# Part of weight 2 moved into the first attention phase, with buffers and first signs re-placed

## The chip, the cores and the metric

The kernel runs on one core of a Trainium2 chip. The metric is device microseconds of one execution, from the first to the last instruction plus what lies around that span. TensorE (PE) multiplies matrices; VectorE (DVE), ScalarE (ACT) and GpSimd (POOL) do the elementwise work; SyncE (SP) issues every DMA of this kernel, plain copies and transposes alike, in one queue. Each engine runs its instructions in the order of its own list and stops at the first whose inputs or buffers aren't ready. "PEld" in the profile is TensorE's weight load.

## The reference, cut to what matters

Three layers in a row, for 2 batches of 768 rows. First an attention of 8 heads of size 64 in which a query sees only the keys of its own hash bucket, then a low-rank token mix with a ReLU layer of 512 to 2048 to 512, then a causal attention by 4 experts with a top-2 gate.

```
q_bits = (q @ proj > 0); k_bits = (k @ proj > 0)          # 6 bits each
mask = bucket(q_bits) == bucket(k_bits)
x = softmax(where(mask, scale * q @ k.T, -1e9)) @ v       # layer 1, heads joined: 512 wide
u = x + (x.T @ U @ V).T
x = u + relu(u @ w_ch1) @ w_ch2                           # layer 2; w_ch1 512 x 2048, w_ch2 2048 x 512
out = sum_e gate_e * (causal_softmax(q_e @ k_e.T) @ v_e @ wo_e)   # layer 3
```

The weights U, V, w_ch1 and w_ch2 arrive as 64-bit floats, which the kernel reads as pairs of 32-bit words.

## The kernel before

Numbers that need more than half precision are kept as two half-precision parts, a high and a low one, so most products take three matmuls.

**Layer 1** goes by pairs of heads (two heads share the 128 partitions), 4 pairs in each batch, and in a pair by 12 tiles of 128 queries x 768 keys: 48 tiles a batch, counted here as tiles 0 to 47 (batch 0) and 48 to 95 (batch 1). In a tile TensorE makes the scores (L607, and L612 with the mask), VectorE takes the row minimum out of PSUM into `P32` (L618), ScalarE takes the exponential (L527), ScalarE or VectorE rounds it to the high half (L529, L531), GpSimd or VectorE subtracts for the low half (L535), SyncE transposes both by DMA into `PT` (L629), and TensorE multiplies with V (L539 to L541). In batch 0 every other tile takes another way: it stays in 32 bits and is transposed on TensorE (`softmax_f32`). The mask comes from sign bits: proj times q and k gives 24 rows of signs for each head, scaled to a large number, which lie in partitions 64 to 87 of `BQ` and `BK` beside the low halves in partitions 0 to 63. `a1_prep` makes the next pair's operands; `a1_first` makes the first pair's by a shorter way: two sign products stand in PSUM partitions 0 to 63, VectorE compares them into `SG` (L516), and SyncE copies 24 rows each to partition 64 and up of `BQ` (L519) and `BK` (L520), for each of the two heads.

**The weights** w_ch1 and w_ch2 come in 16 units each of 128 x 512 numbers. A unit is one DMA of 512 KB (L276), three VectorE operations from 64-bit words to a 32-bit float (L187, L190, L193), one ScalarE operation for the high half (L279) and two on GpSimd for the low half (L280, L281). `w_stream` interleaves the first `NW0` = 16 units (all of weight 1) with tiles 0 to 47 of attention and up to `NW1` = 17 with the 8 tiles after; `need`, called by the first block of the ReLU layer with the numbers in `WAH`, calls for the other 15.

**Space.** Weight 2's place, two tiles of 16 KB a partition (tags `W2_0`, `W2_1`), can't be filled while batch 0's attention runs, since `more_buffers` lends it to attention: 3 further `P32`, 3 `HL`, 2 `PT` and 2 V buffers, besides the 3 each of `P32`, `HL` and `PT` that are there all the time.

**The ReLU layer** (`mlp_stream`) goes by blocks of 256 or 128 rows: 16 products `ph` (L738) with ReLU into `hT` (L739, L740), then 4 products `px` (L758) with weight 2, each followed by a sum on VectorE (L766 to L771). Its blocks of batch 0 are filler for TensorE between the attention tiles of batch 1 (`merge`, `MIX`, `LEAD`).

**The order.** The program text gives priorities; a scheduler with a model of time then writes each engine's list once, when the kernel is built. So an edit of a few lines moves instructions on all engines.

Of the kernel before, what the change touches and what calls it, by code (L numbers as in the profile page):

```python
# [1 line left out]

# [1 line left out]

# [18 lines left out]
def kernel(  # L23
# [17 lines left out]
    nc = tc.nc  # L41
# [30 lines left out]
    IS1 = None
    IS2 = None
    IS3 = None
    IS4 = None
# [5 lines left out]
    W4 = 1.0  # L81
    SOON = 20
    XB = 1
    WAH = (4, 8, 4)
    XNB = 1
    LAGX = 1
    LAGB = 4
# [23 lines left out]
    def halves(n):  # L111
        return [(c, min(512, n - c)) for c in range(0, n, 512)]
# [130 lines left out]


    W1 = [cp.tile([P, ND, FF], FH, name=f"W1_{i}") for i in range(2)]
    W2 = []


    U1 = []
# [54 lines left out]

    M2 = {}
# [36 lines left out]
    def later(n, fn):  # L342
        pending.append([n, fn])
# [113 lines left out]
    def a1_first(b, p):  # L457
# [14 lines left out]
        def turned(src, name):  # L472
# [2 lines left out]
                nc.tensor.transpose(tp[:, t, :], src[:, t, :], identh)  # L475
            return tp

        for j in range(2):
            todo[2 * j]()
            todo[2 * j + 1]()  # L480
            if j == 0:
                load_proj()
        rows = slice(D, D + NR)
        for j in range(2):
            g = slice(NT * j, NT * (j + 1))
            lo = KL[:, :, D * j : D * (j + 1)]
# [12 lines left out]
            tk = turned(KN[:, g], f"tk_{n}_{j}")
            nc.vector.tensor_copy(AK[:, j], tk)  # L500
            tl = turned(lo, f"tl_{n}_{j}")
            nc.scalar.activation(BK[0:D, j], tl, AF.Copy)
            sg = psc.tile([D, 1024], F32, tag="sc", name=f"sg_{n}_{j}")
            for c0, cn in halves(S):
                cs = slice(c0, c0 + cn)
                for last, ops in enumerate((
                    ((PQ, AQ[:, j]), (PK, AK[:, j])),
                    ((PL, AQ[:, j]), (PB[0:D, 0], BK[0:D, j])),
                )):
# [50 lines left out]
    def more_buffers(on):  # L560
        for x in ring.values():
            x.clear()
        if on:
            raw = []
            for i in range(2):
                x = sp.tile([P, 5, S], F32, tag=f"W2_{i}", name=f"more{i}")
                raw += [x[:, j] for j in range(5)]
            half = lambda x, s_: x.bitcast(FH).rearrange("p (a s) -> p a s", s=s_)
            ring["P32"] += raw[0:3]
            ring["HL"] += [half(x, S) for x in raw[3:6]]  # L570
            ring["PT"] += [half(x, P) for x in raw[6:8]]
            VF.extend(x.rearrange("p (t d) -> p t d", d=D) for x in raw[8:10])
# [118 lines left out]
    def a1_stream():  # L691
        pairs = [(b, p) for b in range(B) for p in range(NP)]
        for i, (b, p) in enumerate(pairs):
# [10 lines left out]

            if i == 0:
                later(2, ahead)
                def luv():
                    with tc.issue_after(masked[IS4]) if IS4 is not None else nullcontext():
                        load_uv()
                later(4, luv)  # L710
# [10 lines left out]
    def mlp_stream(b, s0, TB):  # L721
# [350 lines left out]
    def merge(*a):  # L1072
        drain(merged(*a))
# [4 lines left out]

    more_buffers(True)
    a1_first(0, 0)  # L1080
    with tc.issue_after(masked[IS2]) if IS2 is not None else nullcontext():
        for fn in a1_load(0, 1, False):
            fn()

    wunits = [lambda dt=dt, c=c: w1_unit(dt, c) for c in range(FF // 512) for dt in range(ND)]
    wunits += [lambda dt=dt, g=g: w2_unit(dt, g) for dt in range(ND) for g in range(NF // 4)]

    def need(n):
        while given[0] < min(n, len(wunits)):
            with tc.issue_after(masked[IS3]) if IS3 is not None and given[0] < 8 else nullcontext():  # L1090
                wunits[given[0]]()
# [118 lines left out]
```

## Time and profile before

| | us |
|---|---|
| three runs | 654.06, 654.67, 655.4 (median 654.67) |
| profiled execution, whole | 652.22 |
| its span | 650.5 |
| TensorE busy in the span | 577.4 (89%) |
| VectorE busy | 425.9 (65%) |
| ScalarE busy | 347.9 (53%) |
| GpSimd busy | 235.8 (36%) |
| hardware DMA queue, share of 16 engines | 62.3% |

The profile shows one execution. A busy share over the whole span mixes two very different parts: up to about 263 us the attention of layer 1 and the conversion of weights run, with four engines and the DMA much in use; after it TensorE is nearly always busy. So the trace is read by stretches here.

### The profile page before, as it was taken

Reading aid. Unit: us, or ns where it says so; the run is one execution under the profiler, and the core shown is the slowest. Engines: PE = TensorE matmul, PEld = TensorE weight load, DVE = VectorE, ACT = ScalarE, POOL = GpSimd, SP = SyncE. Lnnn points to the kernel's source line nnn. Section 1 sums busy time; section 2 is a strip of 40 time slices with the busy share of each in tenths; the row PEclk is TensorE's granted clock in tenths of the full one; section 3 lists DMA queues with packets and bytes.
Section 4 is the critical chain, followed back from the end, with each engine's and each line's share of the span. In section 5 each row is a group of like instructions: output and inputs, shape, how many; then the busy total and the mean of one; then the engine's idle time right before and its main releaser. Section 6 shows DMA issues by size and latency. Waiting matters only on the chain.

```text
span 650.5 us, 16196 instructions
## 1 busy us (share of the span) xinstructions
PE 577.4 (89%) x6498; PEld 470.1 (72%) x6498; DVE 425.9 (65%) x1030; ACT 347.9 (53%) x744; POOL 235.8 (36%) x215
## 2 busy tenths in 40 slices
PE   5679898796788969989998999999998999998994
PEld 2357677584666659876787888878786888987953
DVE  6886986958978974666765455673772436374295
ACT  4578694865867552684666343452532323354263
POOL 3665776674875773262343200010130000011031
PEclk9999997797999989999999999999998999999998
DMA  8899999969899998495766312251451102026044
GB/s 236 183 208 204 226 219 222 245 134 269 170 230 267 250 217 151 83 195 107 123 122 100 72 30 49 47 108 31 80 89 46 38 10 38 26 46 110 11 100 106
DMA packets 228172, 84.51 MB, mean 130 GB/s; under 512 B 207104, under 2 KB 223616, under 8 KB 228096
## 3 DMA queue, kind: packets, MB, share of 16 engines
q1 hardware_dynamic: 228096, 83.47, 62.3%
q8 instruction: 51, 0.84, 0.5%
q14 instruction: 25, 0.20, 0.1%
HBM read 29.11 MB, written 3.15 MB: 50 GB/s over the span
## 4 chain that ended last, share of the span: by engine, by line
PE 50%; DMA 22%; DVE 10%; POOL 6%; SPq 5%; issue 4%; ACT 3%; DVEq 0%; POOLq 0%; ACTq 0%
DMA PT<-HL 14%; PE ph L738 14%; PE px L758 13%; PE pq L809 2%; PE pk L809 2%; PE s L912 2%; PE po L591 2%; PE pv L841 2%; POOL HL L535 2%; DVE P L618 2%; PE sc L607 2%; DMA more<-HL 1%; SPq L629 1%; PE sc L612 1%; DMA w<-in_moe_w_ch_dram 1%
## 5 line engine op out<-in xcount | busy, mean ns | idle before, releaser
L535 POOL TENSOR_TENSOR HL<-P,HL 128x768 f16<-128x768 f32 (+5 forms) x59 | 86.2, 1462 | 315.7 <-DVE HL L531 180.6
L758 PE MATMUL px<-hT,W 128*128 128x256 f16 (+1 forms) x1344 | 145.2, 259 | 5.1 <-DVE x L766 5.1
L738 PE MATMUL ph<-U,W 128*128 128x256 f16 (+1 forms) x1344 | 144.3, 259 | 0.8 <-DVE hT L740 0.7
L758 PEld LDWEIGHTS <-W 128*128 128x128 f16 x1344 | 115.2, 98 | 20.5 <-issue 6.8
L738 PEld LDWEIGHTS <-W 128*128 128x128 f16 x1344 | 114.9, 98 | 17.1 <-issue 1.9
L527 ACT ACTIVATE P<-P,m 128x768 f32<-128x768 f32 (+5 forms) x103 | 83.0, 806 | 57.1 <-DVE P L920 28.4
L618 DVE TENSOR_SCALAR_CACHE_REDUCE P<-sc 128x768 f32<-128x768 f32 x72 | 68.2, 950 | 12.4 <-PE sc L612 8.7
L740 DVE SCALAR_TENSOR_TENSOR hT<-ph,hT 128x256 f16<-128x256 f32 (+1 forms) x112 | 42.4, 382 | 49.2 <-ACT hT L739 48.6
L539 PEld LDWEIGHTS <-PT 128*128 128x128 f16 x516 | 47.2, 99 | 30.9 <-DMA PT<-HL 25.2
L739 ACT ACTIVATE hT<-ph 128x256 f16<-128x256 f32 (+1 forms) x112 | 38.6, 346 | 57.6 <-PE ph L738 57.0
L529 ACT ACTIVATE HL<-P 128x768 f16<-128x768 f32 (+5 forms) x75 | 56.4, 752 | 18.7 <-DMA PT<-HL 17.7
L607 PE MATMUL sc<-AK,AQ 128*128 128x512 f16 x192 | 50.6, 345 | 14.5 <-DVE more L618 6.2
L539 PE MATMUL po<-V,PT 128*128 128x64 f16 x372 | 41.5, 196 | 12.3 <-DMA PT<-HL 9.0
L612 PE MATMUL sc<-BK,BQ 88*128 88x512 f16 x192 | 50.9, 346 | 0.0
L540 PEld LDWEIGHTS <-PT 128*128 128x128 f16 x516 | 47.2, 99 | 2.0 <-issue 1.1
L541 PEld LDWEIGHTS <-PT 128*128 128x128 f16 x516 | 47.2, 99 | 0.2 <-issue 0.2
L541 PE MATMUL po<-V,PT 128*128 128x64 f16 x372 | 41.5, 195 | 0.0
L540 PE MATMUL po<-V,PT 128*128 128x64 f16 x372 | 41.2, 195 | 0.0
L535 DVE TENSOR_TENSOR HL<-P,HL 128x768 f16<-128x768 f32 (+5 forms) x40 | 34.3, 858 | 9.9 <-ACT HL L529 9.4
L920 DVE TENSOR_SCALAR_CACHE_REDUCE P<-s 128x128 f32<-128x128 f32 (+5 forms) x48 | 29.4, 618 | 10.0 <-PE s L917 9.8
L607 PEld LDWEIGHTS <-AQ 128*128 128x128 f16 x192 | 18.5, 105 | 22.7 <-issue 19.1
L612 PEld LDWEIGHTS <-BQ 88*128 88x128 f16 x192 | 19.7, 103 | 13.9 <-issue 2.8
(238 smaller groups left out, 1181.3 us busy)
## 6 DMA issues: line engine op xcount, KB each, us to landing
w<-in_moe_w_ch_dram SPq DMA_DIRECT2D x16, 512.0 KB
wx<-in_moe_w_ch_dram SPq DMA_DIRECT2D x16, 512.0 KB
qn<-in_q_dram SPq DMA_DIRECT2D x16, 192.0 KB
kn<-in_k_dram SPq DMA_DIRECT2D x16, 192.0 KB
vn<-in_v_dram SPq DMA_DIRECT2D x16, 192.0 KB
out_dram<-o SPq DMA_DIRECT2D x12, 256.0 KB
PT<-HL SPq DMA_TRANSPOSE x99
BQ<-AQ SPq DMA_DIRECT2D x7, 192.0 KB
```

Of the source, the lines that this page charges most:

```text
L527: nc.scalar.activation(P32, P32, AF.Exp, bias=m, scale=-1.0, accum_out=ssum)
L529: nc.scalar.activation(HL[:, 0], P32, AF.Copy)
L535: eng.tensor_tensor(HL[:, 1], P32, HL[:, 0], op=ALU.subtract)
L539: nc.tensor.matmul(o, PT[:, t, :], vh(t), start=(t == 0), stop=False)
L540: nc.tensor.matmul(o, PT[:, t, :], vl(t), start=False, stop=False)
L541: nc.tensor.matmul(o, PT[:, nk + t, :], vh(t), start=False, stop=(t == nk - 1))
L607: nc.tensor.matmul(ps[:, c0 : c0 + cn], aq[:, t, :], ak[:, c0 : c0 + cn], start=True, stop=False,)
L612: nc.tensor.matmul(ps[:, c0 : c0 + cn], bq[:, t, :], bk[:, c0 : c0 + cn], start=False, stop=True,)
L618: nc.vector.tensor_scalar(P32, ps[:, 0:S], CLIP, None, op0=ALU.min, op1=ALU.min, accum_out=m)
L738: nc.tensor.matmul(ph, w, u, start=(i == 0), stop=(i == len(ops) - 1))
L740: nc.vector.scalar_tensor_tensor(hT[1][:, ft, :], ph, 0.0, hT[0][:, ft, :], op0=ALU.max, op1=ALU.subtract)
L758: nc.tensor.matmul(po, w, u, start=(i == 0), stop=(i == len(ops) - 1))
```

## The change

Five edits. (1) In `a1_first` the sign products of q and of k become two products, each written to PSUM partitions 64 to 95, and VectorE compares 24 rows of each straight into `BQ` and `BK`; `SG` and the four copies by DMA are gone. (2) In `a1_prep` the second half of `KN`, a scaled copy, goes from VectorE (L407 before) to GpSimd (L404 after). (3) Weight 2 is split into two pairs of tiles by output column (`W2[0]` and `W2[1]`, 8 units each); the first pair has a place of its own. (4) `more_buffers` lends only the second pair's place and that of `hT`: 2 `P32`, 2 `HL`, 2 `PT` and 2 V buffers. (5) `NWA` = 24 units instead of 16 go with tiles 0 to 47, up to 25 with the next 8 tiles, and the last 7 by `WAH` = (1, 7, 0). The `IS1` to `IS4` switches, all None before, and the place of `load_proj` in the text are clean-up.

```diff
-    WAH = (4, 8, 4)
+    WAH = (1, 7, 0)
...
     def w2_unit(dt, g):
-        if not W2:
-            W2.extend(
-                sp.tile([P, ND, NF, P], FH, tag=f"W2_{i}", name=f"W2_{i}") for i in range(2)
-            )
+        if dt // 2 not in W2:
+            W2[dt // 2] = [
+                sp.tile([P, 2, NF, P], FH, tag=f"W2_{i}_{dt // 2}", name=f"W2_{i}_{dt // 2}")
+                for i in range(2)
+            ]
...
-        nc.vector.tensor_scalar(
-            KN[:, :, D : 2 * D], KN[:, :, 0:D], -0.125, None, op0=ALU.mult
+        nc.gpsimd.tensor_scalar(
+            KN[:, :, D : 2 * D], KN[:, :, 0:D], -0.125, 1.0, op0=ALU.mult, op1=ALU.mult
         )
...
-            sg = psc.tile([D, 1024], F32, tag="sc", name=f"sg_{n}_{j}")
-            for c0, cn in halves(S):
...
-            SG = sp.tile([D, NT, P], FH, tag="KS", bufs=2, name=f"SG_{n}_{j}")
-            nc.vector.tensor_scalar(
-                f2(SG), sg[:, 0:S], thr[0:D, 1:2], far[0:D, 1:2], op0=ALU.is_lt, op1=ALU.mult
-            )
-            nc.sync.dma_start(BQ[rows, j], SG[0:NR])
-            masked.append(nc.sync.dma_start(BK[rows, j], SG[32 : 32 + NR]).ins)
+            for kind, c, ops in (
+                ("q", 1, ((PQ, AQ[:, j]), (PL, AQ[:, j]))),
+                ("k", 0, ((PK, AK[:, j]), (PB[0:D, 0], BK[0:D, j]))),
+            ):
+                sg = psc.tile([P, 1024], F32, tag="sc", name=f"sg{kind}_{n}_{j}")
+                for c0, cn in halves(S):
                     for i, (w, x) in enumerate(ops):
                         nc.tensor.matmul(
+                            sg[D : D + 32, c0 : c0 + cn], w, f2(x)[:, c0 : c0 + cn],
+                            start=(i == 0), stop=(i == 1),
                         )
+                B = BQ if kind == "q" else BK
+                nc.vector.tensor_scalar(
+                    f2(B[rows, j]), sg[rows, 0:S], thr[rows, c : c + 1], far[rows, c : c + 1],
+                    op0=ALU.is_lt, op1=ALU.mult,
+                )
...
-            for i in range(2):
-                x = sp.tile([P, 5, S], F32, tag=f"W2_{i}", name=f"more{i}")
-                raw += [x[:, j] for j in range(5)]
+            for tag in ("W2_0_1", "W2_1_1", "hT0", "hT1"):
+                x = sp.tile([P, 2, S], F32, tag=tag, name=f"more_{tag}")
+                raw += [x[:, j] for j in range(2)]
...
-    NW1 = 17
+    NWA = 24
+    NW1 = 25
...
-    merge(take(a1, NF1), NF1 * CA, w_stream(NW0), NW0)
-    merge(take(a1, PH1 - NF1), (PH1 - NF1) * CA, w_stream(NW1), NW1 - NW0)
+    merge(take(a1, NF1), NF1 * CA, w_stream(NWA), NWA)
+    merge(take(a1, PH1 - NF1), (PH1 - NF1) * CA, w_stream(NW1), NW1 - NWA)
```

Three places in the lists that the scheduler wrote. In them a name such as `w2_3_1` is weight 2's unit of output column block 3 and row group 1 (`_x`, `_32` and `wx` are its staging), `m_1_1_0_5` is the row minimum of batch 1, pair 1, head 0, tile 5, and `us`, `uf`, `vs` belong to the low-rank matrices.

VectorE at the start, from the second sign comparison of the first pair up to tile 0, in the kernel before:

```order
L516 TENSOR_SCALAR SG_0_0_1_243<-sg_0_0_1_234,thr_98,far_99 64x768
L187 TENSOR_SCALAR us_x_416<-us_413 128x192
L190 SCALAR_TENSOR_TENSOR us_x_416<-us_413,us_x_416 128x192
L193 SCALAR_TENSOR_TENSOR uf_415<-us_413,us_x_416 128x192
L208 SCALAR_TENSOR_TENSOR UU1_124<-uf_415,UU0_123 128x6x32
L231 COPY UU0_123<-UU0_123 128x6x32 x2
L231 COPY UU1_124<-UU1_124 128x6x32 x2
L402 SCALAR_TENSOR_TENSOR QN_0_1_329<-QN_0_1_329,qn_0_1_252 128x12x64
L407 TENSOR_SCALAR KN_0_1_330<-KN_0_1_330 128x12x64
L187 TENSOR_SCALAR vs0_x_431<-vs0_426 96x384
L618 TENSOR_SCALAR more0_128,m_0_0_0_0_269<-sc_0_0_0_0_264 128x768
```

The same stretch in the changed kernel, from the first sign comparison:

```order
L512 TENSOR_SCALAR BQ_0_0_140<-sgq_0_0_0_193,thr_98,far_99 24x768
L512 TENSOR_SCALAR BK_0_0_141<-sgk_0_0_0_199,thr_98,far_99 24x768
L184 TENSOR_SCALAR w1_0_0_x_298<-w1_0_0_64_295 128x512
L496 COPY AK_0_0_139<-tk_0_0_1_219 128x768
L512 TENSOR_SCALAR BQ_0_0_140<-sgq_0_0_1_235,thr_98,far_99 24x768
L187 SCALAR_TENSOR_TENSOR w1_0_0_x_298<-w1_0_0_64_295,w1_0_0_x_298 128x512
L512 TENSOR_SCALAR BK_0_0_141<-sgk_0_0_1_241,thr_98,far_99 24x768
L190 SCALAR_TENSOR_TENSOR w1_0_0_32_296<-w1_0_0_64_295,w1_0_0_x_298 128x512
L612 TENSOR_SCALAR more_W2_0_1_128,m_0_0_0_0_269<-sc_0_0_0_0_264 128x768
```

Four comparisons of 24 rows stand where two of 64 rows stood, and tile 0 (L618, now L612) follows the last of them with one weight operation between; the low-rank matrices, `QN` and `vs` come behind tile 0, and `KN` has left the list.

VectorE at tile 67 (`m_1_1_1_1`) and the first sum of the ReLU layer (`x2_0_0_0`), before:

```order
L618 TENSOR_SCALAR P32_1_1_1_1_3685,m_1_1_1_1_3684<-sc_1_1_1_1_3679 128x768
L190 SCALAR_TENSOR_TENSOR w2_3_1_x_3008<-wx0_293,w2_3_1_x_3008 128x512
L535 TENSOR_TENSOR HL_1_1_0_5_3563<-P32_1_1_0_5_3561,HL_1_1_0_5_3563 128x768
L193 SCALAR_TENSOR_TENSOR wx0_293<-wx0_293,w2_3_1_x_3008 128x512
L187 TENSOR_SCALAR w2_3_2_x_3018<-w2_3_2_64_3015 128x512
L402 SCALAR_TENSOR_TENSOR QN_1_3_3965<-QN_1_3_3965,qn_1_3_3196 128x12x64
L190 SCALAR_TENSOR_TENSOR w2_3_2_x_3018<-w2_3_2_64_3015,w2_3_2_x_3018 128x512
L407 TENSOR_SCALAR KN_1_3_3966<-KN_1_3_3966 128x12x64
L193 SCALAR_TENSOR_TENSOR w2_3_2_32_3016<-w2_3_2_64_3015,w2_3_2_x_3018 128x512
L766 SCALAR_TENSOR_TENSOR x2_0_0_0_3114<-px_0_0_0_3033,U_0_0_796 128x256
```

And in the changed kernel:

```order
L184 TENSOR_SCALAR w2_3_3_x_3034<-wx1_294 128x512
L187 SCALAR_TENSOR_TENSOR w2_3_3_x_3034<-wx1_294,w2_3_3_x_3034 128x512
L612 TENSOR_SCALAR P32_1_1_1_0_3646,m_1_1_1_0_3645<-sc_1_1_1_0_3640 128x768
L190 SCALAR_TENSOR_TENSOR wx1_294<-wx1_294,w2_3_3_x_3034 128x512
L612 TENSOR_SCALAR P32_1_1_1_1_3693,m_1_1_1_1_3692<-sc_1_1_1_1_3687 128x768
L757 SCALAR_TENSOR_TENSOR x2_0_0_0_3122<-px_0_0_0_3041,U_0_0_815 128x256
L529 TENSOR_TENSOR HL_1_1_0_5_3571<-P32_1_1_0_5_3569,HL_1_1_0_5_3571 128x768
L760 TENSOR_TENSOR x2_0_0_0_3122<-x2_0_0_0_3122,U_0_1_816 128x256
L399 SCALAR_TENSOR_TENSOR QN_1_3_3973<-QN_1_3_3973,qn_1_3_3204 128x12x64
L762 TENSOR_TENSOR U_0_1_816<-x2_0_0_0_3122,U_0_0_815 128x256
```

The first sum stood behind tile 67 by five weight operations, a subtraction (`HL`) and the next pair's `QN` and `KN`; now it stands right behind tile 67, ahead of that subtraction and of `QN`, and all of weight 2 has been converted. Counted on VectorE's lists, 16 units have been begun by tile 47 before and 22 now, and 32 by the end in both.

GpSimd at the second pair's preparation, before:

```order
L412 TENSOR_TENSOR KL_0_1_331<-kn_0_1_253,KN_0_1_330 128x6x64 x2
L452 TENSOR_SCALAR more1_129<-vn_0_1_254 128x768
L454 TENSOR_TENSOR V_0_1_337<-more1_129,V_0_1_337 128x768
L535 TENSOR_TENSOR more0_128<-more0_128 128x768 x2
L535 TENSOR_TENSOR more1_129<-P32_0_0_0_4_463,more1_129 128x768
L412 TENSOR_TENSOR KL_0_2_738<-kn_0_2_354,KN_0_2_737 128x6x64 x2
```

And now:

```order
L449 TENSOR_SCALAR more_hT1_131<-vn_0_1_254 128x768
L404 TENSOR_SCALAR KN_0_1_330<-KN_0_1_330 128x12x64
L409 TENSOR_TENSOR KL_0_1_331<-kn_0_1_253,KN_0_1_330 128x6x64 x2
L529 TENSOR_TENSOR more_W2_1_1_129<-more_W2_0_1_128,more_W2_1_1_129 128x768
L451 TENSOR_TENSOR V_0_1_337<-more_hT1_131,V_0_1_337 128x768
L277 TENSOR_SCALAR wx0_293<-wx0_293 128x512
```

`KN` stands in front of `KL`, which SyncE's transposes of K wait for, and the first of the low halves (`more_W2`) comes directly behind.

## Rows read from the trace of the kernel before

**Rows 1.** Page, part 1: busy time, share of the span, instructions.

```profile
PE 577.4 (89%) x6498; PEld 470.1 (72%) x6498; DVE 425.9 (65%) x1030; ACT 347.9 (53%) x744; POOL 235.8 (36%) x215
```

**Rows 2.** Windows: stretch, length, busy by engine, clock, DMA share, GB/s.

```profile
23.00:157.00 134.00, 113.48 (x1141) 88.81 (x1141) 106.55 (x208) 94.54 (x175) 86.39 (x72) 0.92 1.01 213
157.00:263.00 106.00, 88.96 (x1057) 71.74 (x1055) 83.28 (x155) 64.20 (x122) 68.75 (x59) 0.98 1.01 211
263.00:650.50 387.50, 362.50 (x4246) 303.99 (x4243) 220.79 (x620) 179.46 (x434) 70.45 (x55) 0.99 0.39 74
```

**Rows 3.** Windows of 20 us around the first ReLU block, same columns.

```profile
160.00:180.00 20.00, 15.35 (x210) 12.20 (x208) 18.45 (x35) 17.37 (x33) 17.93 (x15) 1.00 0.89 179
200.00:220.00 20.00, 17.38 (x186) 12.87 (x186) 17.72 (x35) 13.56 (x28) 13.67 (x13) 1.00 1.12 267
220.00:240.00 20.00, 14.40 (x164) 12.42 (x162) 15.95 (x27) 9.15 (x15) 13.52 (x14) 0.96 1.09 232
240.00:260.00 20.00, 20.00 (x248) 17.86 (x247) 11.13 (x20) 6.73 (x13) 9.05 (x8) 0.95 0.98 162
```

**Rows 4.** Timeline, start: start us, length, engine, line, operation, out<-in, [idle<-releaser].

```profile
9.43 0.61 PE L511 MATMUL sg<-AQ,PQ 128*32 128x512 f16 x1 [2.02 <-DVE PQ L177]
...
9.83 0.63 PE L511 MATMUL sg<-AQ,PL 128*32 128x512 f16 x1
...
12.72 1.07 DVE L516 TENSOR_SCALAR SG<-sg,thr,far 64x768 f16<-64x768 f32 x1
...
15.10 0.90 SPq L519 DMA_DIRECT2D BQ<-SG  x1
...
17.42 1.07 DVE L516 TENSOR_SCALAR SG<-sg,thr,far 64x768 f16<-64x768 f32 x1 [1.84 <-PE sg L511]
...
20.72 0.95 DVE L402 SCALAR_TENSOR_TENSOR QN<-QN,qn 128x768 f16<-128x768 f16 x1
...
23.03 0.94 DVE L618 TENSOR_SCALAR_CACHE_REDUCE more<-sc 128x768 f32<-128x768 f32 x1
```

**Rows 5.** Groups by line, VectorE, 23-157 us: xcount, busy us, mean ns, idle.

```profile
L190 DVE SCALAR_TENSOR_TENSOR w_x<-wx,w_x 128x512 uint32<-128x512 uint32 x8 | 5.5, 693 | 0.1
...
L407 DVE TENSOR_SCALAR KN<-KN 128x768 f16<-128x768 f16 x4 | 3.0, 742 | 0.0
```

**Rows 6.** The same for GpSimd, 23 to 157 us.

```profile
L281 POOL TENSOR_TENSOR W<-wx,W 128x512 f16<-128x512 f32 x7 | 8.1, 1160 | 0.4
...
L280 POOL TENSOR_SCALAR w<-w 128x512 f32<-128x512 f32 x7 | 4.3, 617 | 12.9 <-ACT W L279 12.8
...
L452 POOL TENSOR_SCALAR more<-vn 128x768 f32<-128x768 f32 x3 | 2.5, 830 | 3.7 <-PE po L591 3.5
```

**Rows 7.** Waits, 23-157 us: waiter, releaser, total us, times, longest.

```profile
DVE w_x L187 <- DMA w<-in_moe_w_ch_dram: 6.8, 5, 3.6
```

**Rows 8.** Waits, 157 to 263 us.

```profile
ACT HL L529 <- DMA PT<-HL: 16.2, 12, 3.5
...
PE px L758 <- DVE x L766: 5.1, 1, 5.1
...
DVE P L618 <- POOL HL L535: 3.3, 2, 2.2
```

**Rows 9.** Timeline, VectorE: tiles 47, 67 and 68, and the first MLP sum.

```profile
156.90 0.95 DVE L618 TENSOR_SCALAR_CACHE_REDUCE P<-sc 128x768 f32<-128x768 f32 x1
...
229.78 0.96 DVE L618 TENSOR_SCALAR_CACHE_REDUCE P<-sc 128x768 f32<-128x768 f32 x1
...
234.10 0.96 DVE L535 TENSOR_TENSOR HL<-P,HL 128x768 f16<-128x768 f32 x1 [2.74 <-ACT HL L529]
...
238.62 0.42 DVE L766 SCALAR_TENSOR_TENSOR x<-px,U 128x256 f32<-128x256 f32 x1
...
262.96 0.96 DVE L618 TENSOR_SCALAR_CACHE_REDUCE P<-sc 128x768 f32<-128x768 f32 x1
```

**Rows 10.** Line L407: count, shortest/median/longest ns, first and last start.

```profile
L407 DVE TENSOR_SCALAR KN<-KN x7: 354/679/1384, 21.6 to 237.8; 128x768 f16<-128x768 f16 x7
```

More of the change, by code (lines that the diff above doesn't have):

```diff
@@ L1 @@
-from contextlib import ExitStack, nullcontext
+from contextlib import ExitStack
 import numpy as np
@@ L71 @@
     XV = False
[L72 to L75, printed above, removed]
+    LUV = 4
     PJ = nc.vector
@@ L245 @@
     W1 = [cp.tile([P, ND, FF], FH, name=f"W1_{i}") for i in range(2)]
-    W2 = []
+    W2 = {}
     U1 = []
@@ L301, in w2_unit @@
             ],
-            [w[:, dt, 4 * g : 4 * g + 4, :] for w in W2], 16.0, f"w2_{dt}_{g}",
+            [w[:, dt % 2, 4 * g : 4 * g + 4, :] for w in W2[dt // 2]], 16.0, f"w2_{dt}_{g}",
         )
@@ L384 @@
     preps = {}
-    masked = []
     def a1_prep(b, p, wait):
@@ L476, in turned @@
             return tp
+        load_proj()
         for j in range(2):
@@ L480, in a1_first @@
             todo[2 * j + 1]()
-            if j == 0:
-                load_proj()
         rows = slice(D, D + NR)
@@ L502, in a1_first @@
             nc.scalar.activation(BK[0:D, j], tl, AF.Copy)
-            sg = psc.tile([D, 1024], F32, tag="sc", name=f"sg_{n}_{j}")
-            for c0, cn in halves(S):
[L505 to L509, printed above, removed]
+            for kind, c, ops in (
[4 more added lines that the diff above has]
+                for c0, cn in halves(S):
                     for i, (w, x) in enumerate(ops):
                         nc.tensor.matmul(
-                            sg[32 * i : 32 * (i + 1), cs], w, f2(x)[:, cs],
-                            start=(last == 0), stop=(last == 1), skip_group_check=True,
-                        )
-            SG = sp.tile([D, NT, P], FH, tag="KS", bufs=2, name=f"SG_{n}_{j}")
-            nc.vector.tensor_scalar(
-                f2(SG), sg[:, 0:S], thr[0:D, 1:2], far[0:D, 1:2], op0=ALU.is_lt, op1=ALU.mult
-            )
-            nc.sync.dma_start(BQ[rows, j], SG[0:NR])
-            masked.append(nc.sync.dma_start(BK[rows, j], SG[32 : 32 + NR]).ins)
-        with tc.issue_after(masked[IS1]) if IS1 is not None else nullcontext():
-            todo[4]()
-            todo[5]()
+                            sg[D : D + 32, c0 : c0 + cn], w, f2(x)[:, c0 : c0 + cn],
+                            start=(i == 0), stop=(i == 1),
+                        )
+                B = BQ if kind == "q" else BK
[3 more added lines that the diff above has]
+                )
+        todo[4]()
+        todo[5]()
         a1_values(b, p, vn, V)
@@ L564, in more_buffers @@
             raw = []
-            for i in range(2):
-                x = sp.tile([P, 5, S], F32, tag=f"W2_{i}", name=f"more{i}")
-                raw += [x[:, j] for j in range(5)]
+            for tag in ("W2_0_1", "W2_1_1", "hT0", "hT1"):
+                x = sp.tile([P, 2, S], F32, tag=tag, name=f"more_{tag}")
+                raw += [x[:, j] for j in range(2)]
             half = lambda x, s_: x.bitcast(FH).rearrange("p (a s) -> p a s", s=s_)
[L569 to L572, printed above, removed]
+            ring["P32"] += raw[0:2]
+            ring["HL"] += [half(x, S) for x in raw[2:4]]
+            ring["PT"] += [half(x, P) for x in raw[4:6]]
+            VF.extend(x.rearrange("p (t d) -> p t d", d=D) for x in raw[6:8])
     def softmax_f32(P32, m, ssum, o, vf, v0, n, t, mode):
@@ L706, in a1_stream @@
                 later(2, ahead)
[L707 to L710, printed above, removed]
+                later(LUV, load_uv)
             else:
@@ L728, in mlp_stream @@
             if b == 0 and s0 == 0:
-                need(NW0 + WAH[0] + WAH[1] * ft // NF)
+                need(NWA + WAH[0] + WAH[1] * ft // NF)
             fs = slice(P * ft, P * (ft + 1))
@@ L745, in mlp_stream @@
             if b == 0 and s0 == 0:
-                need(min(NW0 + WAH[0] + WAH[1] + WAH[2] * (dt + 1), 2 * NW0))
+                need(min(NWA + WAH[0] + WAH[1] + WAH[2] * (dt + 1), 2 * NW0))
             po = mm_tile([P, TB], F32, f"px_{n}_{dt}")
             ops = [
-                (W2[i][:, dt, ft, :], hT[jj][:, ft, :])
+                (W2[dt // 2][i][:, dt % 2, ft, :], hT[jj][:, ft, :])
                 for ft in range(NF)
@@ L1080 @@
     a1_first(0, 0)
-    with tc.issue_after(masked[IS2]) if IS2 is not None else nullcontext():
-        for fn in a1_load(0, 1, False):
-            fn()
+    for fn in a1_load(0, 1, False):
+        fn()
     wunits = [lambda dt=dt, c=c: w1_unit(dt, c) for c in range(FF // 512) for dt in range(ND)]
@@ L1089, in need @@
         while given[0] < min(n, len(wunits)):
-            with tc.issue_after(masked[IS3]) if IS3 is not None and given[0] < 8 else nullcontext():
-                wunits[given[0]]()
+            wunits[given[0]]()
             given[0] += 1
```

## The prediction

> **What bounds the kernel now.** I read the page first, for the whole [rows 1]: TensorE is busy for 577.4 of 650.5 us, so 73 us are idle, and no other engine is near its limit. Then the windows, to see where the idle time lies. I cut the span at three events on VectorE's timeline [rows 4, 9]: the row minimum of tile 0 (23.03), of tile 47 (156.90) and of tile 68 (262.96). Stretch A, 23 to 157 us, is batch 0's attention with all of weight 1; stretch B, 157 to 263, holds 20 tiles of batch 1, the first ReLU block and weight 2; the rest follows. The reader is to see in [rows 2] that A leaves TensorE 134.0 - 113.5 = 20.5 us idle and B 106.0 - 89.0 = 17.0, while the 387.5 us after 263 leave only 25.0. In A and B nothing is full by itself: VectorE is at 79.5% and 78.6%, GpSimd at 64% and 65%, while DMA stands at 1.01 in both. They are bound by four engines and one DMA queue that wait for one another in fixed lists. So work added there costs less than its length, and work taken away gives less.
>
> Third, the waits. In A, VectorE stood 6.8 us at weight words that hadn't landed, 5 times [rows 7]. In B, TensorE stood 5.1 us at once because the first ReLU sum was late on VectorE [rows 8]; the timeline [rows 9] shows how: behind tile 67 the list goes through weight operations, stops 2.74 us at an `HL` subtraction, goes through more weight operations and the next pair's `QN` and `KN`, and reaches the sum only at 238.62. The window 220 to 240 shows it from TensorE's side: 14.40 of 20 us busy, between 17.38 before and 20.00 after [rows 3].
>
> **The start (S).** The first pair's signs end with two comparisons of 1.07 us and four DMAs, the first issued at 15.10 for 0.90 us of SyncE's time [rows 4]. Now tile 0 waits for four comparisons and no DMA. TensorE first: q and k products share a column group now, so they run one after the other. Products of 512 columns in one group started 0.40 us apart (9.43 and 9.83), so I take 0.40 for 512 and 0.20 for 256. q needs 2 x 0.40 + 2 x 0.20 = 1.2, ending at 10.6, with one k product between 11.1; k's rest comes after the second half's transposes, at about 13. VectorE: comparison of q to 12.2, of k from 13.0 to 14.0, then by its new list three weight operations (0.6 apart), a copy (0.5) and two comparisons (2.1): 18.4. Tile 0's minimum then starts at about 18.5 instead of 23.03, 4.5 earlier. What stood before it is not gone: `us`, `UU`, `QN` and `vs`, some 3.5 us, come behind tile 0, and I charge them to A. Bounds: VectorE idled 3.5 us between 9 and 23 and gains two comparisons of 1.07, so on work alone 1.4 is won; at most 5, with tile 0 at 18. I take 4.0, near the count. It counts the four DMAs too, of which each takes 0.7 to 0.9 us of SyncE.
>
> **Stretch A.** By tile 47, 22 units are begun instead of 16. Each costs VectorE 3 x 0.69 = 2.07 [rows 5], so +12.4. `KN` leaves: 4 x 0.74 = -3.0. With the 3.5 from the start VectorE's work goes from 106.6 to 119.4. At its present share of 79.5% that takes 150.2 us, +16.2; if all fits into its 27.5 idle us, nothing. Between them: VectorE was busy for 18.45 and 17.72 of 20 us in two windows of B [rows 3], 90%, under the same mixture of tiles and units. I take 86%, below these, since GpSimd takes on 6 x (1.16 + 0.62) = 10.7 and five `KN` of about 0.83 (its nearest row is a scaling of the same 768 columns [rows 6]), 4.2, and goes from 86.4 to 101 of 139, 73%. 119.4 / 0.86 = 138.8: **+4.8**. SyncE issues six more loads. Fewer lent buffers (5 instead of 6 `P32` and `HL`, 5 `PT` as before) I cost at nothing: batch 1 runs on three, at a tile's `P32` wait of 3.3 us in all of B [rows 8]. If five were short, the price would be of that size. `hT`'s place is free in time: the first ReLU needs the joined heads of batch 0, which need the last tile that uses it.
>
> **Stretch B.** 10 units instead of 16 remain, 6 x 2.07 = 12.4 less on VectorE, and two `KN`, 1.5; GpSimd and the loads lose six units too. VectorE falls from 83.3 to 69.4, so it no longer holds the pace. TensorE's 89.0 remain: at 97% busy, as the window 240 to 260 shows it can be with ReLU work at hand [rows 3], B takes 91.7, -14.3; if only other waits come up, 0. What I can name is the 5.1 us wait: in the new list the sum stands right behind tile 67, ahead of the `HL` that stopped it. Of the other 11.9 idle us I take a sixth, 1.9, because 16.2 us of ScalarE's waits in B are for buffers that a transposing DMA still read [rows 8], with three `HL` for 20 tiles, which stay three. **-7.0**.
>
> **After 263 us** TensorE's list is the same from tile 68 on, and it is 94% busy; nothing there, give or take 1. `KN` for the last pair is on GpSimd at 18% there [rows 2].
>
> Sum: -4.0 + 4.8 - 7.0 = -6.2. The profiled execution took 652.22 in all (650.5 of span), so 646.0 for it; the median of the runs is 654.67, 2.45 above, so **648.5** for a median.
>
> **A rule that speaks against edit 2.** The same `KN` instruction lasted from 354 to 1384 ns on VectorE [rows 10]; something other than its size sets that. The Trainium skill, page "Perfetto Trace Analysis", section "Optimizing Scalar/DVE Operations", says that GpSimd and VectorE share an SBUF read port, held exclusively, so moving work between the two may not help. By that rule the spread is waiting at the port, which the trace allows but doesn't prove. The sum by it would leave out the 3.0 us that A is credited with.
>
> **Rivals.**
> - *A grows at its own share (slower).* Each unit puts three operations into VectorE's list, and the first stops the list until its words have landed; [rows 7] has 5 such stops in 15 units, the longest 3.6 us, with DMA at 1.01. With six units more and the tiles closer packed the stops keep their share: +16.2 in A, S and B as above: 654.7 - 4.0 + 16.2 - 7.0 = 659.9. It decides from A's growth of 11 us on. For it: A and B are equally loaded, so moved work should cost what it gives. Against: VectorE at 90% in B.
> - *The same at half price (no change).* A +10.5, the middle of 4.8 and 16.2: 654.2.
> - *B at TensorE's pace (faster still).* All 14.3 are won: 654.7 - 4.0 + 4.8 - 14.3 = 641.2. For it: 20.00 of 20 us in 240 to 260, right after the last units. Against: the transposes' waits in B.
> - *`KN` on GpSimd holds VectorE as long as it did itself.* The credit of 3.0 goes: A's work is 122.4, at 86% 142.3, +8.3: 652.0. For it: the spread in [rows 10]. Against: on GpSimd it is one instruction in front of `KL`, which waited for ScalarE anyway. The rule above says this.
>
> That the change doesn't do what it says I give no chance: the lists show the units and the sum where it puts them.
>
> **How the numbers follow.** Forecast 0.50, with its own range of 644 to 652; slower 0.18; no change 0.13; B at TensorE's pace 0.12; `KN` 0.07. The range 639 to 658 takes in the lower rival with S at its best bound, and the upper one up to A's growth of about 14; outside are some 0.09 above and 0.05 below. A difference under 0.2% (1.3 us) can't be told from none here. Faster: 0.50 + 0.12 + 0.07 = 0.69; same 0.13; slower 0.18.
>
> **What would show it.** S: tile 0's minimum at 18 to 19 us, no mask copies in SyncE's list. A: tile 47's minimum 18.5 + 138.8 = about 157, or later than 163 if the slower rival holds, and VectorE's wait for weight words not over 10 us. B: no TensorE wait of several us for the first ReLU sum, and tile 68 some 6 us before 263. Rest: 387 us from tile 68 to the end. I am wrong if tile 68 comes later than 262, or if the rest of the run changes by more than 2 us.

## The result, and the profile after

The changed kernel takes **649.02 us** (median of four runs, 648.1 to 650.05) beside 655.03 (654.06 to 655.87) for the kernel before in the same series: the ratio is 0.9899, with a 95% interval of 0.9864 to 0.9933. The forecast was 648.5. The profiled execution took 648.14 us, with a span of 646.4.

By stretches, from the start of row minimum to row minimum (tile 0, 47 and 68), in us:

| stretch | before | after | change | forecast |
|---|---|---|---|---|
| start, up to tile 0 | 23.03 | 18.49 | -4.5 | -4.0 |
| A, tiles 0 to 47 | 133.9 | 140.8 | +6.9 | +4.8 |
| B, tiles 47 to 68 | 106.1 | 100.0 | -6.1 | -7.0 |
| from tile 68 to the end | 387.5 | 387.2 | -0.4 | 0 |
| sum | 650.5 | 646.4 | -4.1 | -6.2 |

The page's first part of the profile after, which answers to [rows 1]:

```profile
PE 579.1 (90%) x6498; PEld 472.5 (73%) x6498; DVE 426.7 (66%) x1025; ACT 348.5 (54%) x744; POOL 242.7 (38%) x222
```

No engine's busy time shrank; GpSimd's grew by 7 us, most of it the seven `KN`. The same three stretches as in [rows 2] (stretch, length, then busy time of TensorE, its weight load, VectorE, ScalarE and GpSimd, granted clock, DMA share, GB/s):

```profile
18.50:159.25 140.75, 117.14 (x1141) 91.03 (x1140) 119.82 (x231) 100.07 (x184) 105.58 (x92) 0.88 1.05 227
159.25:259.24 99.99, 87.51 (x1057) 71.44 (x1056) 73.32 (x136) 61.48 (x116) 59.73 (x49) 1.00 1.01 196
259.24:646.40 387.16, 362.56 (x4246) 303.88 (x4244) 219.96 (x621) 179.62 (x434) 70.54 (x55) 0.99 0.39 74
```

The third column is VectorE: 119.82 us of work in A, where the forecast said 119.4, at 85% of the stretch, where it said 86%. In B TensorE is idle for 12.5 us instead of 17.1, and its own work takes 1.5 us less, at a granted clock of 1.00 (2.4 GHz) instead of 0.98. The last stretch is as it was.

The start, from VectorE's timeline, answers to [rows 4]:

```profile
10.15 1.07 DVE L512 TENSOR_SCALAR BQ<-sgq,thr,far 24x768 f16<-24x768 f32 x1
12.02 1.07 DVE L512 TENSOR_SCALAR BK<-sgk,thr,far 24x768 f16<-24x768 f32 x1 [0.79 <-PE sgk L507]
...
14.94 1.07 DVE L512 TENSOR_SCALAR BQ<-sgq,thr,far 24x768 f16<-24x768 f32 x1 [0.54 <-PE sgq L507]
...
16.77 1.07 DVE L512 TENSOR_SCALAR BK<-sgk,thr,far 24x768 f16<-24x768 f32 x1
17.88 0.69 DVE L190 SCALAR_TENSOR_TENSOR w<-w,w_x 128x512 uint32<-128x512 uint32 x1
18.49 0.95 DVE L612 TENSOR_SCALAR_CACHE_REDUCE more_W<-sc 128x768 f32<-128x768 f32 x1
```

A comparison of 24 rows lasts 1.07 us, as one of 64 rows did. Four of them stand in the row, tile 0 follows at 18.49, and no copy by DMA lies between.

The first ReLU sum in VectorE's list, beside [rows 9]:

```profile
227.26 0.68 DVE L190 SCALAR_TENSOR_TENSOR wx<-wx,w_x 128x512 uint32<-128x512 uint32 x1
229.98 0.96 DVE L612 TENSOR_SCALAR_CACHE_REDUCE P<-sc 128x768 f32<-128x768 f32 x1 [2.04 <-POOL HL L529]
230.87 0.08 DVE L612 DVE_READ_ACCUMULATOR P<-sc 128x1 f32 x1
230.87 0.42 DVE L757 SCALAR_TENSOR_TENSOR x<-px,U 128x256 f32<-128x256 f32 x1
```

The last weight operation is done before tile 67, and the sum (L757) stands right behind that tile, at 230.87 instead of 238.62. The wait of TensorE for it, 5.1 us in [rows 8], is gone: the largest of TensorE's waits in B are now these (waiter, releaser, total us, times, longest):

```profile
PE po L533 <- DMA PT<-HL: 3.9, 6, 1.3
PE sg L431 <- DVE P L612: 2.3, 1, 2.3
PE sg L431 <- DMA AQ<-QN: 1.9, 1, 1.9
```

and the 20 us windows of [rows 3] show the same from its side:

```profile
200.00:220.00 20.00, 15.28 (x163) 11.59 (x161) 17.47 (x34) 13.55 (x28) 12.12 (x12) 1.00 1.18 256
220.00:240.00 20.00, 20.00 (x213) 16.93 (x211) 14.47 (x24) 10.08 (x18) 15.49 (x14) 1.00 0.96 184
240.00:260.00 20.00, 20.00 (x276) 18.11 (x275) 8.53 (x15) 5.52 (x11) 2.48 (x2) 1.00 0.90 147
```

From 220 us on TensorE never stops (20.00 of 20), where it had 14.40. The 20 us before that are weaker than they were: 15.28 against 17.38 in [rows 3].

### The profile page after: what moved, and what is told of

Same layout as the page of the kernel before. It is cut to its first block, busy times and chain, and to the rows that moved or that the text cites. A ratio compares the mean times of both kernels' runs of the same rounds, so it can differ in the third digit from the quotient of the medians.

```text
span 646.4 us, 16197 instructions
## 1 busy us (share of the span) xinstructions
PE 579.1 (90%) x6498; PEld 472.5 (73%) x6498; DVE 426.7 (66%) x1025; ACT 348.5 (54%) x744; POOL 242.7 (38%) x222
## 4 chain that ended last, share of the span: by engine, by line
PE 52%; DMA 17%; DVE 11%; POOL 7%; issue 6%; ACT 4%; SPq 2%; DVEq 0%; POOLq 0%; ACTq 0%
PE px L749 15%; PE ph L729 12%; DMA PT<-HL 11%; PE pq L800 2%; DMA PT<-more_W 2%; PE pk L800 2%; PE po L585 2%; POOL HL L529 2%; DVE P L612 2%; PE s L903 2%; PE pv L832 2%; PE sc L601 1%; PE sc L606 1%; PE sg L431 1%; ACT P L521 1%
## 5 line engine op out<-in xcount | busy, mean ns | idle before, releaser
L529 POOL TENSOR_TENSOR HL<-P,HL 128x768 f16<-128x768 f32 (+5 forms) x64 | 93.7, 1464 | 320.0 <-DVE HL L525 182.8
L521 ACT ACTIVATE P<-P,m 128x768 f32<-128x768 f32 (+5 forms) x109 | 88.7, 814 | 57.7 <-DVE P L911 28.9
L612 DVE TENSOR_SCALAR_CACHE_REDUCE P<-sc 128x768 f32<-128x768 f32 x76 | 71.8, 950 | 12.5 <-PE sc L606 8.0
L523 ACT ACTIVATE HL<-P 128x768 f16<-128x768 f32 (+5 forms) x80 | 60.6, 757 | 15.3 <-DMA PT<-HL 14.1
L529 DVE TENSOR_TENSOR HL<-P,HL 128x768 f16<-128x768 f32 (+5 forms) x40 | 35.6, 889 | 9.6 <-ACT HL L523 9.2
```

The costliest lines, as they stand in the source:

```text
L521: nc.scalar.activation(P32, P32, AF.Exp, bias=m, scale=-1.0, accum_out=ssum)
L523: nc.scalar.activation(HL[:, 0], P32, AF.Copy)
L529: eng.tensor_tensor(HL[:, 1], P32, HL[:, 0], op=ALU.subtract)
L612: nc.vector.tensor_scalar(P32, ps[:, 0:S], CLIP, None, op0=ALU.min, op1=ALU.min, accum_out=m)
```

## The experiments

Two questions were open: whether each term of the sum is earned by the part that it was given to, and how much of the result is the order of the lists. Each kernel was timed in five rounds beside the kernel before, whose own median moved from series to series: 657.04 beside the next four kernels (signs alone to no move), 654.9 beside `KN` back, signs with `KN` and the first re-ordering of each kernel, 657.29 beside the rest. The ratios allow for that and the microseconds don't; the times expected were set against 655.

**Signs alone.** The kernel before with edit 1:

```diff
-            SG = sp.tile([D, NT, P], FH, tag="KS", bufs=2, name=f"SG_{n}_{j}")
...
-            masked.append(nc.sync.dma_start(BK[rows, j], SG[32 : 32 + NR]).ins)
+                nc.vector.tensor_scalar(
+                    f2(B[rows, j]), sg[rows, 0:S], thr[rows, c : c + 1], far[rows, c : c + 1],
+                    op0=ALU.is_lt, op1=ALU.mult,
+                )
```

> The kernel before with edit 1 alone (the first pair's signs written at the mask rows' partitions, no copies). Theory of the sum: tile 0's minimum starts 4 to 5 us earlier than 23.0 and that lasts, so about 651 against 655; the 5 us wait of TensorE for the first ReLU sum stays. Rival 'start only' (the move of weight units gives back what it costs, so the start is all of the gain): 649. Rival 'move only' (the head start is used up in the first attention phase, which is paced by the engines' work): 655, with tile 47's minimum still at about 157 us.

Measured: 662.91, ratio 1.0093 (1.0055 to 1.0131), 0.9% slower, which is clear of the noise and which no theory expected. Tile 0 starts at 18.5, as forecast, but A is 140.1 and B 118.8. The lead of 4.5 us is gone by the end of A: tile 47 stands at 158.56, 1.7 us later than before. Its windows from 220 us on show what happens in B, which is 12.7 us longer:

```profile
220.00:230.00 10.00, 10.00 (x88) 8.31 (x85) 8.91 (x17) 5.11 (x10) 7.01 (x8) 0.94 1.10 260
230.00:240.00 10.00, 6.36 (x99) 5.02 (x96) 7.26 (x10) 3.64 (x6) 6.21 (x7) 1.00 1.21 279
240.00:250.00 10.00, 1.84 (x36) 1.56 (x36) 9.52 (x15) 5.57 (x9) 8.87 (x9) 0.59 0.94 240
250.00:260.00 10.00, 7.00 (x51) 5.33 (x52) 5.99 (x11) 2.09 (x4) 7.63 (x8) 0.56 0.90 188
```

TensorE is busy for 1.84 of 10 us, while VectorE (9.52) and GpSimd (8.87) are nearly full. Its waits in this kernel's stretch B:

```profile
PE po L537 <- DMA PT<-HL: 18.0, 9, 4.1
PE px L756 <- DVE wx L193: 2.8, 1, 2.8
```

and GpSimd's timeline in the hole:

```profile
237.07 1.21 POOL L280 TENSOR_SCALAR wx<-wx 128x512 f32<-128x512 f32 x1
238.36 1.15 POOL L281 TENSOR_TENSOR W<-wx,W 128x512 f16<-128x512 f32 x1
239.59 0.62 POOL L280 TENSOR_SCALAR w<-w 128x512 f32<-128x512 f32 x1
240.30 1.16 POOL L281 TENSOR_TENSOR W<-w,W 128x512 f16<-128x512 f32 x1
242.18 1.65 POOL L533 TENSOR_TENSOR HL<-P,HL 128x768 f16<-128x768 f32 x1 [0.72 <-ACT HL L527]
...
247.59 1.63 POOL L533 TENSOR_TENSOR HL<-P,HL 128x768 f16<-128x768 f32 x1
```

At the place where the second products `px` of the ReLU layer begin, TensorE has two kinds of work left. `px` lacks converted weights: VectorE finishes the ones it waits for at 254.1 (the 2.8 us wait). The attention tiles ahead of it wait for `PT`; these waits ended at 235.6, 240.9, 245.7 and 250.2, one in about 5 us. The chain of work that ended last, as the profile infers it, leads to the last of them through these pieces (start, length, what):

```profile
225.13 7.31 DMA PT<-HL
...
233.38 1.65 POOL HL L533
...
237.07 1.22 POOL wx L280
...
239.37 4.19 DMA kn<-in_k_dram
...
243.92 6.26 DMA PT<-HL
```

Two transposes make up 13.6 us of these 25 us, a load of K 4.2, and GpSimd's weight operations (235.11 to 238.28) 3.0. GpSimd's list has up to three weight units between one `HL` and the next, but at 242.18 it stood idle for ScalarE's high half before it could subtract. So late weights explain why `px` can't fill TensorE; that they hold the attention tiles too isn't shown. I call this place **the hole**; I read the 5.1 us wait in [rows 8] as its shape in the kernel before.

**Without signs; the move alone.** The changed kernel with the old form of `a1_first`, once with edit 2 and once with `KN` on VectorE:

```diff
-        nc.gpsimd.tensor_scalar(
-            KN[:, :, D : 2 * D], KN[:, :, 0:D], -0.125, 1.0, op0=ALU.mult, op1=ALU.mult
+        nc.vector.tensor_scalar(
+            KN[:, :, D : 2 * D], KN[:, :, 0:D], -0.125, None, op0=ALU.mult
```

> The changed kernel with edits 1 and 2 undone: only weight 2's split, the buffers in the ReLU layer's place and the moved units remain. Theory of the sum: first attention phase 5 to 7 us longer than the 134 of before, the stretch with the first ReLU block 6 to 8 us shorter, so about 653 to 654, and no wait of several us for the first ReLU sum. Rival 'start only': 655. Rival 'move only': 649.

> The changed kernel with edit 1 alone undone. Theory of the sum: 649 + 4 = 653, tile 0's minimum back at about 23 us. Rival 'start only': 655. Rival 'move only': 649.

Measured: the move alone (edits 3 to 5) 654.19, ratio 0.9946 (0.992 to 0.9972), near the sum's 653 to 654 (by the ratio a little better than that); with `KN` on GpSimd as well 664.04, 1.0097 (1.0061 to 1.0134), 11 us above the sum's 653, or 8 by the ratio. The first has tile 0 at 22.0, A 142.5, B 100.2 and 388.0 to the end: the move costs A 8.6 us and gives B 5.9. By these profiled runs it wins nothing (a span of 652.7 against 650.5); the 0.5% is one of medians, since the profiled run of before was one of its quickest. The second has B 108.5, without a hole; in its trace some 20 more `ph` products stand ahead of tile 68 (274 against 254).

**No move.** The changed kernel with the unit counts of before, so with edits 1 to 4:

```diff
-    WAH = (1, 7, 0)
+    WAH = (4, 8, 4)
...
-    NWA = 24
-    NW1 = 25
+    NWA = 16
+    NW1 = 17
```

> The changed kernel with the counts of weight units as before (16 with tiles 0 to 47, 17 by tile 55, the rest by 4, 8, 4); weight 2 stays split and the buffers stay as changed. Theory of the sum: 649 + 2 = 651: the first attention phase shrinks by 5 to 7 us, the ReLU block's stretch grows by 7 to 8 and has its wait for the first sum again. Rival 'start only': 649. Rival 'move only': 655.

Measured: 658.96, 1.0018 (0.9984 to 1.0051). By the ratio that is the rival 'move only' (655, a ratio of 1) and not the sum's 651. A is 131.8, shorter than before with one `P32` and one `HL` fewer. B is 119.1, 19.1 us longer than in the changed kernel where the sum had 7 to 8, and the waits for `PT<-HL` are like those of signs alone:

```profile
PE po L533 <- DMA PT<-HL: 17.3, 10, 3.0
```

**`KN` back on VectorE** in the changed kernel (the diff above), and **signs with `KN`** but no move in the kernel before:

> The changed kernel with edit 2 alone undone: KN is scaled on VectorE again; signs and moved units stay. The sum credits KN's move with 3 us, so 652. If the difference between the two runs without the signs edit (KN on GpSimd 10 us slower than on VectorE) were the price of the KN instruction itself, 640. If that difference came of the order that the scheduler wrote and not of the instruction, 647 to 652, with tile 0 at 18 to 19 us and no TensorE gap of 10 us where the first ReLU block's second products begin.

> The kernel before with edits 1 and 2, no weight units moved. Theory of the gap: without the move the ReLU block's second products stand without their weights and can't fill TensorE between tiles 64 and 68, so the gap of the signs-only run (8 of 10 us idle at 240 to 250) comes again: 656 to 664. If the signs-only run was slower by its own list's bad luck and not by that gap: 650 to 654.

Measured: 656.25, 1.0018 (0.9987 to 1.0048), and 656.85, 1.0026 (0.9998 to 1.0054). The second met the theory of the hole: TensorE 2.28 of 10 us in 230 to 240, B 119.5. It differs from the list without the move only in weight 2's split and the buffers: A is 130.7 against 131.8, so no large price of the smaller loan is seen; one pair can't tell it to 1 us, since the order alone moves A by more (below). The first met none of its expected times. With `KN` on GpSimd, three pairs that differ in that alone come out 1.2% faster (changed kernel against `KN` back), 0.7% faster (signs with `KN` against signs alone) and 1.5% slower (without signs against the move alone). In A the three agree: it is 3.0, 9.3 and 0.6 us shorter with `KN` on GpSimd. They part in B, which is 5.9 shorter, 0.7 longer and 8.3 longer. One edit with effects of both signs points at the lists, so the next runs moved no work at all.

The parts don't add up either: signs alone 1.0093, the move alone 0.9946, both of them (`KN` back) 1.0018, all five edits 0.9899.

**The same work in another order.** `AHEAD` is a distance that the scheduler looks ahead. With another value the instructions are the same and stand in another order.

```diff
-    AHEAD = 40
+    AHEAD = 30
```

(30 and 44 for the kernel before; 36, 30 and 44 for the changed one.)

> A control: the kernel before with one priority number (AHEAD) at 30 instead of 40, so the same instructions in another order from about tile 20 on. If single edits can be read to 2 us: 653 to 657. If the scheduler's order alone moves the time by as much as the edits did, it lies outside that, by 3 to 8 us, and single-edit runs must be read by their stretches, not by their totals.

> The same control for the changed kernel: AHEAD at 36 instead of 40, same instructions, another order from about tile 14 on. If single edits can be read to 2 us: 647 to 651. If not: outside it by 3 to 8 us. In either case by the theory of the gap no TensorE gap of 10 us stands where the first ReLU block's second products begin, since weight 2's first half is there.

> The kernel before with the scheduler's AHEAD at 44 instead of 40: the same instructions, written in another order. Theory (the move closes a gap): as in the five lists so far whose units are not moved, TensorE is busy for about half or less of some 10 us between 210 and 260, tile 68 starts about 110 to 120 us after tile 47, and the time lies at 653 to 659. Rival (the order of the list decides, whatever is moved): no such gap, B near 100, time below 651.

> The changed kernel with AHEAD at 30 instead of 40, the same instructions in another order. Theory: no 10 us between 210 and 260 with TensorE under 6.5 us busy, tile 0 at 16 to 19, A of 139 to 144, B of 100 to 107, time 648 to 654. Rival (the changed kernel's gain is the luck of one list): B over 110, time 655 or more.

> The changed kernel with AHEAD at 44 instead of 40, the same instructions in another order. Theory: no 10 us between 210 and 260 with TensorE under 6.5 us busy, tile 0 at 16 to 19, A of 139 to 144, B of 100 to 107, time 648 to 654. Rival (luck of one list): B over 110, time 655 or more.

Measured, with the stretches of the profiled runs and the least that TensorE was busy in any 10 us that start between 220 and 250:

| list | us | ratio (95%) | tile 0 | A | B | least PE |
|---|---|---|---|---|---|---|
| before, 40 | 655.03 | 1 | 23.0 | 133.9 | 106.1 | 4.85 |
| before, 30 | 656.29 | 1.0017 (0.999-1.0043) | 21.2 | 137.2 | 112.8 | 2.79 |
| before, 44 | 660.49 | 1.0036 (1.0003-1.007) | 22.2 | 138.3 | 108.6 | 4.69 |
| changed, 40 | 649.02 | 0.9899 (0.9864-0.9933) | 18.5 | 140.8 | 100.0 | 10.00 |
| changed, 36 | 652.6 | 0.9974 (0.994-1.0007) | 18.1 | 139.5 | 106.5 | 8.92 |
| changed, 30 | 645.86 | 0.9835 (0.9799-0.9871) | 18.6 | 136.0 | 103.8 | 9.79 |
| changed, 44 | 654.4 | 0.9972 (0.9946-0.9999) | 18.4 | 142.4 | 103.5 | 9.36 |

(The last one's profiled run, 660.57, lies 6 us above its median; it took 394.6 us after tile 68, where the others took 385.6 to 389.5.) The times of the changed kernel missed their bounds by 1.6 us (36), 2.1 below (30) and 0.4 (44), that of before with 44 by 1.5; taken by the ratio, the two with 44 lie within theirs, and 36 and 30 miss by 2.3 and 3.8. The stretches came as expected but for A with 30, 3 us shorter, and B of before with 44, 1.4 shorter.

Two things follow. An order that changes no work moves the changed kernel by 1.4% (0.9835 to 0.9974), more than the largest term of the sum (7.0 us, 1.1%); so a total of one list says little about one edit. And the means of the lists come near the sum: tile 0 at 18.4 against 22.2 (-3.8), A 139.7 against 136.5 (+3.2), B 103.4 against 109.2 (-5.7). The rest, forecast at 0, is 1.5 us longer in these means, by the one run of 394.6.

The hole sorts all kernels by the move alone. These are the two weakest windows of a kernel with 16 units by tile 47 and the two weakest of one with more (of the kernel before with signs, of the one with signs and `KN`; `KN` back, and without signs):

```profile
238.00:248.00 10.00, 1.84 (x36) 1.56 (x36) 9.65 (x15) 5.44 (x9) 8.87 (x10) 0.69 1.14 278
```

```profile
230.00:240.00 10.00, 2.28 (x36) 1.97 (x36) 6.82 (x10) 5.10 (x10) 6.03 (x7) 0.50 1.11 281
```

```profile
220.00:230.00 10.00, 7.17 (x83) 5.39 (x82) 9.26 (x19) 6.73 (x13) 9.13 (x8) 1.00 1.18 224
```

```profile
220.00:230.00 10.00, 7.53 (x76) 6.20 (x75) 4.88 (x11) 6.30 (x12) 8.76 (x7) 0.93 1.16 193
```

All six lists without the move lie at 1.84 to 4.85 us, all eight with it at 7.17 to 10.00. The gap is widest for these starts: if windows from 200 us on are taken in, it is 1.84 to 4.85 against 5.89 to 7.79 (the changed kernel's weakest, 5.89, is 208 to 218). So the move goes with the closing of the hole in every list. By what, these runs leave open: in the changed kernel it takes six conversions and six loads of 512 KB out of B at once, and no run parts the two. Nor are VectorE and GpSimd full in every hole: in the second of these windows they are at 6.82 and 6.03 of 10.

**Fewer units moved.** The changed kernel with 20 instead of 24:

```diff
-    WAH = (1, 7, 0)
+    WAH = (2, 7, 2)
...
-    NWA = 24
-    NW1 = 25
+    NWA = 20
+    NW1 = 21
```

> The changed kernel with 20 units with tiles 0 to 47 instead of 24 (21 with the next 8, and WAH (2, 7, 2)). Theory (A grows with the units moved, the gap before the first px closes as soon as enough are converted): A some 3 to 4 us shorter than in the changed kernel (about 137), B between 100 and 110; 647 to 652, so it may beat the changed kernel by a little if 20 units are enough. Rival (the gap needs all of the first half of weight 2): a gap of half-busy TensorE for 10 us remains, B 110 or more, 653 to 658.

Measured: **644.44** (642.51 to 647.67), ratio 0.9815 (0.9775 to 0.9854), the fastest of all. Its three stretches:

```profile
17.30:152.10 134.80, 115.16 (x1118) 88.82 (x1115) 112.45 (x217) 97.72 (x181) 96.52 (x82) 0.87 1.02 210
152.10:258.00 105.90, 88.52 (x1072) 72.54 (x1072) 82.19 (x149) 63.03 (x120) 71.23 (x59) 0.98 1.03 214
258.00:642.80 384.80, 360.61 (x4255) 302.60 (x4253) 219.02 (x622) 179.91 (x434) 68.20 (x55) 1.00 0.41 76
```

VectorE has 7.4 us less work in A than in the changed kernel and A is 6.0 shorter, B as much longer, with no window under 8.79 us of those in the table; tile 0 comes 1.2 earlier and the end 2.4 nearer to tile 68. So the first theory's B and hole hold, its A is 2 us too long and its time, 647 to 652, too long as well. It beats both kernels in the form they have, but the changed kernel's list with `AHEAD` 30 lies at 0.9835, within its interval: that 20 units are better than 24, and not only this list luckier, isn't shown.

## Why the prediction was right, point by point

*What bounds.* Right. A follows VectorE: its work came out at 119.8 us against 119.4, and between 24 and 20 units A went with it (7.4 us of work, 6.0 of time). But the order counts too: the three lists of before have 106.6 to 107.6 us of that work in an A of 133.9 to 138.3.

*The start, -4.0.* The size is right, and the best borne out: -4.5, and tile 0 stands at 16.3 to 18.6 in all nine lists with edit 1 and at 21.2 to 23.5 in the five without. On the way there the second comparison ended at 13.09, 0.9 us before its place in the forecast, and a wait of 0.54 us for TensorE and weight operations of 0.70 us instead of 0.6 took most of that back. But what an earlier tile 0 is worth depends on the rest. The forecast's own sum charges the 3.5 us of work that moves behind tile 0 to A, where at 86% they are worth 4.1, as much as the start wins; so by that sum edit 1 alone was worth nothing, which the 651 expected for it left out. With signs alone the lead was indeed gone by tile 47. In the two lists that have edit 1 and `KN` on GpSimd but no move it was still there (tile 47 at 148.6 and 149.2), and was lost at the hole (B 119.5 and 119.1).

*A, +4.8.* The size was off: +6.9. The work was 0.4 us more, worth 0.5, and the share 85.1% instead of 86%, worth 1.4. In the means over lists it is +3.2, so the miss is within what an order does. The slower rival's mechanism, more stops for weight words, did not come: VectorE waited for them 5.5 us in A, against 6.8 in [rows 7], with six units more:

```profile
DVE w_x L184 <- DMA w<-in_moe_w_ch_dram: 4.1, 3, 2.6
...
DVE w_x L184 <- DMA wx<-in_moe_w_ch_dram: 1.4, 1, 1.4
```

*Buffers at nothing.* Not contradicted: of the two kernels that differ only in them and weight 2's split, A is 131.8 and 130.7, a difference smaller than what an order does.

*B, -7.0.* The 5.1 us wait went as named; of the 1.9 expected from others none came, since TensorE's idle time fell by 4.6, and 1.5 came from its shorter busy time instead. What the forecast missed is that this place is the hole: it read the wait as one sum standing late in one list. In the lists without the move it shows up as the wait for the first sum (5.1 and 5.3 us, `AHEAD` 40 and 44) or for `PT<-HL` (12.0 to 19.3 us, the four others). That the two kinds of wait have one cause is a reading of these six lists; no run shows it.

*`KN`.* The duration was right: 0.83 us for most, against 0.74 on VectorE. All seven on GpSimd, beside `QN` on VectorE after (line L399, count, shortest, median and longest ns):

```profile
L404 POOL TENSOR_SCALAR KN<-KN x7: 827/832/1416, 22.2 to 236.8; 128x768 f16<-128x768 f16 x7
```

```profile
L399 DVE SCALAR_TENSOR_TENSOR QN<-QN,qn x7: 948/951/1614, 21.4 to 233.8; 128x768 f16<-128x768 f16 x7
```

Spreads remain on both engines. In the three pairs that differ in edit 2 alone VectorE's busy time falls by 5.6, 5.4 and 7.5 us, and its seven `KN` had lasted 5.5 together, so the rival that `KN` holds VectorE from GpSimd isn't seen. (From before to changed VectorE's busy time grew by 0.8 us, where seven `KN` out and two comparisons in would make it some 3 less. Other operations lasted longer in this list; why, no run shows.) The Trainium skill, page "Perfetto Trace Analysis", section "Optimizing Scalar/DVE Operations", says that moving work between these two may not help, since they share a read port. The busy time of VectorE here gives no sign of it, and the totals, with effects of both signs, can't decide it. In A, where the forecast put its 3.0 us, all three pairs have the forecast's sign, but by 0.6 to 9.3 us. Whether edit 2 helps as a whole stays open.

*The rest, 0.* Right: -0.4.

*From the sum to the median.* The sum was 2.1 us too good for the profiled execution (646.0 against 648.14). The median came within 0.5, because the profiled run of before lay 2.45 below its median and that of after only 0.88: 1.6 us of the closeness are this luck. And the order of the lists alone spreads the changed kernel over 8.5 us, as wide as the forecast's own range of 644 to 652. The sign is borne out by the families, with all four lists of the changed kernel under the three of before (for one of them, 36, the interval reaches 1.0007); the last microseconds aren't.

## What to carry to other kernels

Where a scheduler writes the lists, time two or three re-orderings of the same work before a single edit's total is believed, and read each edit in its own stretch, where it can be told. A wait that is read as one late instruction may be a place where the engine has nothing else that is ready: look what it could do instead, and what that waits for. An earlier start is worth its microseconds only if the next place of scarcity has been widened as well.

## What the runs showed of the hardware that was not expected

The hole of signs alone cost TensorE more than its idle time, since the granted clock fell with it. Little ran on it from 234 us on; the clock went from 1.00 (2.4 GHz) to 0.50 (1.2 GHz), stood there from 244 to 256 us, and rose again while `px` ran without a stop. Windows of four microseconds of that kernel:

```profile
240.00:244.00 4.00, 0.70 (x18) 0.58 (x18) 3.93 (x7) 3.15 (x6) 3.11 (x4) 0.72 1.06 269
244.00:248.00 4.00, 1.14 (x18) 0.98 (x18) 3.72 (x7) 1.89 (x4) 3.92 (x5) 0.50 1.15 298
...
252.00:256.00 4.00, 1.86 (x9) 1.28 (x9) 3.35 (x6) 1.05 (x2) 3.75 (x4) 0.50 1.08 205
256.00:260.00 4.00, 4.00 (x26) 3.01 (x24) 1.94 (x4) 0.42 (x1) 2.05 (x3) 0.65 0.89 195
```

`px` products of the same shape lasted 273 ns before the hole, 333 ns on average for the 52 behind it, and 273 again from 262 us on. The comparison of 24 rows that takes as long as one of 64 (1.07 us) shows that on VectorE only the row's length counted here, which is why four comparisons cost two more than two did.
